# Half-block units in the first batch, an early 256 token filler job and a paced filler

## The chip, the cores and the metric

The kernel runs on one core of one Trainium2 chip. The core has TensorE (PE in the profile; PEld is its weight load), VectorE (DVE), ScalarE (ACT), GpSimd (POOL) and SyncE (SP), which here only issues DMAs. The metric is the device time of one execution in microseconds.

## The reference

Three layers, one after the other, on float32 data: windowed attention with a linear distance bias (4 batches, 8 heads, 576 tokens, head size 64, window 128), a gated layer with a 1536 wide inner dimension, and a layer with a cosine gate, 2048 wide inside. The model width is 512, the tokens are 2304.

```python
scores = scale * q @ k.T ;  mask = (rel >= 0) & (rel < 128)
attn = softmax(where(mask, scores - slope[h] * abs(rel), -1e9))
x = (attn @ v)                                  # to 2304 x 512
g = x @ w_gate ; x = (silu(g) * (x @ w_val)) @ w_out
h = x @ w_in2 ;  out = (h * cos(h)) @ w_out2
```

## The kernel before

Products of the two later layers are made of three matmuls of a high and a low part (`mm3`, lines 80 to 83, and 972 to 974), 128 rows deep, with the tokens as columns. The inputs come as 64 bit floats; each weight tile is converted on the core (`convert`, lines 100 to 177: ScalarE lines 127 and 129, VectorE 130, 137, 138, 142, GpSimd or ScalarE for the high part, GpSimd 164 for the low part).

**Attention** is a loop over item slots `n` (lines 638 to 702). A unit is a pair of heads of one batch, 16 units in all, four to a batch (`NP`). A unit has nine items: two heads times four blocks of 128 queries, and one item for the last 64 tokens of both heads (`i == NB`). Items go through stages at fixed lags in slots: scores (`do_s`, PE line 473), bias and row minimum (`do_bias`, VectorE 481), exponential (`do_exp`, ScalarE 490), reciprocal of the sum (VectorE 496, 501), scaling (`do_norm`, GpSimd 514), transposition (`do_t`, PE 533 or 523), copy of the transposed block (`do_hi`, ScalarE 551 or VectorE 554, 555), the product with v (`do_pv`, PE 587, tail 565 and 567). The result goes to `xh` and `xl` (ScalarE 592, 574; VectorE 593, 576), 512 tokens at a time, the tail separately. Two items at a time make a group. Every engine works through its instructions in the order in which this loop gives them out; `post` holds what is given out one slot later.

Units are prepared one ahead: q and k of the next unit are transposed on PE through the one bank `pq` (line 410, also used by the tail of the product with v), copied out by VectorE (416) and ScalarE (419, 430, 432). Their loads (line 352, 357) and those of v (368, 372) are issued by SyncE in the order of the loop; v's tile has two buffers, so a load of v waits in SyncE's queue for the unit two before.

**The filler** puts the first part of the gated layer, 3 of its 12 column tiles (`F0`), between attention work. When the last unit of a batch is done, `release(b)` (line 291) is called, which happens at slot 42 for batch 0. `filler` then yields one step of three matmuls at a time, two jobs of 288 tokens for each batch. A job has 12 gate steps, 12 value steps (`a_l1`, evacuations in lines 238 to 264) and 12 output steps (`a_l2`, written out by line 284), with the output steps of a job behind the gate steps of the next. `run_fill` takes 1.6 steps a slot (`RATE`). What is left after the attention stage runs in lines 976 to 983.

**After that** come the rest of the gated layer (lines 1019 to 1047) and the cosine layer (lines 1179 to 1217). In the latter, each product bank is emptied by `take` (VectorE line 1113, ScalarE 1123), and `slot_chains` moves each living chain (`cosine`, lines 1084 to 1104) one step: ScalarE, a VectorE pair (1091, 1092), ScalarE, GpSimd 1097, ScalarE, a subtraction (1103). In the first three steps `take` stands ahead of the chains.

## Time and profile before

| | us |
|---|---|
| median of 3 runs | 991.73 |
| lowest, highest | 990.09, 994.07 |
| the profiled execution | 992.14 |
| its span, first to last instruction | 990.4 |
| mean granted TensorE clock in it | 0.987 |

The profile is of one execution. Busy time of an engine is the time in which it has an instruction under way; matmuls overlap, so a busy PE need not be at its peak, and the granted clock (1.00 is 2.4 GHz, 0.50 is 1.2 GHz, values between are means over both) says how fast it ran. The views used are the page (busy time, slices), windows (busy time by stretch), timelines of one engine, groups of instructions and the issues of DMAs. In a timeline the bracket gives the idle time of the engine ahead of the instruction and what ended it.

### The profile page before, as it was taken

The page shows a single profiled execution, that of the slowest core. Times are in us where ns is not written, and L with a number is a line of the kernel's source. Part 1 is how long each engine was busy: PE and PEld are TensorE (multiplying, and loading weights), DVE is VectorE, ACT ScalarE, POOL GpSimd, SP SyncE. Part 2 cuts the span into 40 slices and gives each one's busy share as a digit, 9 for nine tenths or more (in the row PEclk, how much of TensorE's full clock was granted, in tenths as well). Part 3 has the DMA queues.
Part 4 walks back from the last instruction along what each step waited for, and adds up shares of the span by engine and source line. Part 5 has one row for each costly group of instructions (what it writes and reads, how often), then busy time and mean ns, then how long its engine had stood idle before and what let it go on. Part 6 is the DMA issues. An engine that isn't in the chain of part 4 may idle for free.

```text
span 990.4 us, 17037 instructions
## 1 busy us (share of the span) xinstructions
PE 967.4 (98%) x5616; PEld 887.2 (90%) x5616; DVE 737.3 (74%) x1548; ACT 594.4 (60%) x1365; POOL 483.1 (49%) x567
## 2 busy tenths in 40 slices
PE   6789999999999999999999999999999999999998
PEld 4558888889999999999999999888889888898886
DVE  6867777766288989989989755789666796666664
ACT  6876676644254545555455433877677776776663
POOL 5656556652245667769678721544222342223221
PEclk9879999999999999999999999999999999999999
DMA  7642333322383647547557525865767656676552
GB/s 180 154 98 61 97 81 77 84 80 70 107 282 107 203 128 232 194 137 249 168 171 243 195 91 173 281 198 183 242 199 230 199 163 199 187 240 201 165 176 85
DMA packets 145159, 163.65 MB, mean 165 GB/s; under 512 B 64688, under 2 KB 105648, under 8 KB 144816
## 3 DMA queue, kind: packets, MB, share of 16 engines
q1 hardware_dynamic: 143872, 162.27, 52.6%
q8 instruction: 45, 0.74, 0.3%
q10 hardware_dynamic: 1200, 0.30, 0.1%
q14 instruction: 42, 0.34, 0.1%
HBM read 126.88 MB, written 35.65 MB: 164 GB/s over the span
## 4 chain that ended last, share of the span: by engine, by line
PE 93%; DVE 2%; ACT 1%; issue 1%; POOL 1%; SPq 1%; DMA 1%; POOLq 0%; DVEq 0%
PE l L81 13%; PE l L83 13%; PE l L82 13%; PE pm L81 9%; PE pm L82 8%; PE pm L83 8%; PE pm L972 5%; PE pm L974 5%; PE pm L973 5%; PE s L473 4%; PE pv L587 3%; PE pq L410 1%; PE t L533 1%; PE t L523 1%; DVE r L1092 1%
## 5 line engine op out<-in xcount | busy, mean ns | idle before, releaser
L1097 POOL TENSOR_TENSOR r<-r,c 128x384 f32<-128x384 f32 x96 | 104.6, 1091 | 250.9 <-ACT r L1095 171.2
L81 PE MATMUL pm<-xh,wh 128*128 128x384 f32 (+1 forms) x452 | 151.7, 336 | 0.0
L83 PE MATMUL pm<-xh,wl 128*128 128x384 f32 (+1 forms) x452 | 144.9, 321 | 0.0
L82 PE MATMUL pm<-xl,wh 128*128 128x384 f32 (+1 forms) x452 | 144.9, 320 | 0.0
L81 PE MATMUL l<-wo,hh 128*128 128x512 f32 x288 | 114.0, 396 | 0.0
L82 PE MATMUL l<-wo,hh 128*128 128x512 f32 x288 | 113.5, 394 | 0.0
L83 PE MATMUL l<-wo,hl 128*128 128x512 f32 x288 | 113.5, 394 | 0.0
L972 PE MATMUL pm<-xh,ws 128*128 128x384 f32 x318 | 107.8, 339 | 0.8 <-DVE q L1113 0.7
L793 POOL TENSOR_TENSOR cs<-cs,st 128x512 uint32<-128x512 uint32 x56 | 80.3, 1433 | 56.6 <-DVE cs L791 47.0
L974 PE MATMUL pm<-xh,ws 128*128 128x384 f32 x318 | 107.7, 339 | 0.0
L973 PE MATMUL pm<-xl,ws 128*128 128x384 f32 x318 | 107.2, 337 | 0.0
L514 POOL TENSOR_SCALAR e<-e,st 128x128 f32<-128x128 f32 (+1 forms) x144 | 60.2, 421 | 60.3 <-DVE st L501 45.0
L81 PEld LDWEIGHTS pm<-xh,wh 128*128 128x128 f32 x452 | 85.3, 189 | 3.6 <-issue 3.0
L82 PEld LDWEIGHTS pm<-xl,wh 128*128 128x128 f32 x452 | 85.4, 189 | 0.0
L83 PEld LDWEIGHTS pm<-xh,wl 128*128 128x128 f32 x452 | 85.2, 188 | 0.0
L1087 ACT ACTIVATE a<-c 128x384 f32<-128x384 f32 x96 | 49.7, 517 | 53.2 <-DVE c L1113 53.2
L490 ACT ACTIVATE e<-e,st 128x256 f32<-128x256 f32 (+1 forms) x144 | 68.0, 474 | 18.8 <-DVE st L481 13.5
L1092 DVE SCALAR_TENSOR_TENSOR r<-a,r 128x384 f32<-128x384 f32 x96 | 76.8, 800 | 3.3
L1094 ACT ACTIVATE r<-r 128x384 f32<-128x384 f32 x96 | 50.4, 525 | 44.0 <-DVE r L1092 43.9
L81 PE MATMUL l<-uh,wh 128*128 128x384 f32 x216 | 72.8, 337 | 0.2 <-DVE acc L918 0.2
L83 PE MATMUL l<-uh,wl 128*128 128x384 f32 x216 | 72.6, 336 | 0.0
L82 PE MATMUL l<-ul,wh 128*128 128x384 f32 x216 | 72.5, 336 | 0.0
(179 smaller groups left out, 2624.0 us busy)
## 6 DMA issues: line engine op xcount, KB each, us to landing
ws<-wid SPq DMA_DIRECT2D x168, 256.0 KB, 2.8
wo<-wod SPq DMA_DIRECT2D x48, 512.0 KB, 4.8
st<-in_moe_w_out_dram SPq DMA_DIRECT2D x28, 512.0 KB, 3.8
st<-in_moe_w_in_dram SPq DMA_DIRECT2D x16, 512.0 KB, 3.8
st<-in_moe_w_gate_dram SPq DMA_DIRECT2D x12, 512.0 KB, 4.0
st<-in_moe_w_val_dram SPq DMA_DIRECT2D x12, 512.0 KB, 4.0
wid<-sh SPq DMA_DIRECT2D x24, 256.0 KB, 4.2
wid<-sl SPq DMA_DIRECT2D x24, 256.0 KB, 4.0
```

The lines of the kernel that those rows point to most:

```text
L81: nc.tensor.matmul(out=ps, lhsT=ah, rhs=bh, start=start, stop=False)
L82: nc.tensor.matmul(out=ps, lhsT=ah, rhs=bl, start=False, stop=False)
L83: nc.tensor.matmul(out=ps, lhsT=al, rhs=bh, start=False, stop=stop)
L490: nc.scalar.activation(out=e[:, :w], in_=e[:, :w], func=AF.Exp, bias=st[:, m:m + 1], scale=-1.0, accum_out=st[:, 2 + 2 * m:3 + 2 * m])
L514: nc.gpsimd.tensor_scalar(e[:, :w], e[:, :w], st[:, 8 + 2 * m:9 + 2 * m], 1.0, ALU.mult, ALU.mult)
L793: nc.gpsimd.tensor_tensor(out=ti, in0=ti, in1=st[:, :, 0], op=ALU.add)
L972: nc.tensor.matmul(out=o, lhsT=wh, rhs=xh_, start=start and kk == 0, stop=False, skip_group_check=True)
L973: nc.tensor.matmul(out=o, lhsT=wh, rhs=xl_, start=False, stop=False, skip_group_check=True)
L974: nc.tensor.matmul(out=o, lhsT=wl, rhs=xh_, start=False, stop=kk == 1, skip_group_check=True)
L1092: nc.vector.scalar_tensor_tensor(out=r, in0=a, scalar=-C2, in1=r, op0=ALU.mult, op1=ALU.add)
L1094: nc.scalar.activation(out=r, in_=r, func=AF.Abs)
L1097: nc.gpsimd.tensor_tensor(out=r, in0=r, in1=h, op=ALU.mult)
```

## The change

In batch 0, units 1, 2 and 3 are cut in two: blocks 0 and 1 of the three units come first (items 9 to 20), then blocks 2 and 3 with the tail (items 21 to 35). The number of items and slots stays. The product with v of a half covers only its columns, 256 tokens at a time, and a unit's chunk is marked in `ready` when the first 256 tokens are there. The filler's first job has 256 tokens and begins with two gate tiles at once, chunk by chunk as `ready` says; the last chunk comes at item 29, after which it goes on with gate and value steps, and with output steps if all its inputs are there. The second job of batch 0 has the other 320 tokens and waits for the release. `rate` spreads the steps that are left up to the next release.

The lags for transposing, copying and the product with v become 4, 5 and 6 slots for the first halves and unit 3, and 5, 6 and 7 for the second halves of units 1 and 2. Loads and preparation get slots of their own (`Q0`, `K0`, `TT0`, `LQ`, `LV`); units 2 and 3 are loaded and prepared earlier. The tiles for v, q, k and the tails have four buffers. The tail product of units 2 and 3 goes to the pool `pm` (before, that of unit 3 alone). In the cosine layer, `take` of steps 0 to 2 moves behind the chains, as in the later steps, and the subtraction of step 0 moves from GpSimd to VectorE.

```diff
+    ready = set()
     def a_l1(job, nm, fs, st):
-        b, hf = job
-        tok = slice(b * S + hf * HT, b * S + (hf + 1) * HT)
+        t0, nt = job
+        tok = slice(t0, t0 + nt)
+        if t0 == 0 and nm == "g":
+            two = [bank() for _ in range(2)]
+            for kk in range(KD):
+                while kk not in ready or ("g", 1) not in g0:
+                    yield "wait"
+                c = slice(kk * 128, (kk + 1) * 128)
+                for f in range(2):
+                    wh, wl = g0["g", f]
+                    mm3(two[f][:, :nt], wh[:, c], wl[:, c], xh[:, kk, tok], xl[:, kk, tok], kk == 0, kk == KD - 1)
+                    if kk == KD - 1:
+                        post.append(lambda f=f: evac_l1("g", f, st, two[f], nt))
+                    yield
+            fs = fs[2:]
...
-                mm3(ps[:, :HT], wh[:, c], wl[:, c], xh[:, kk, tok], xl[:, kk, tok], kk == 0, kk == KD - 1)
+                mm3(ps[:, :nt], wh[:, c], wl[:, c], xh[:, kk, tok], xl[:, kk, tok], kk == 0, kk == KD - 1)
                 if kk == KD - 1:
-                    post.append(lambda ps=ps, f=f: evac_l1(nm, f, st, ps))
+                    post.append(lambda ps=ps, f=f: evac_l1(nm, f, st, ps, nt))
...
     def filler():
         prev = None
         for b in range(B):
-            while released[0] < b:
-                yield "wait"
-            for hf in range(2):
+            cut = HA if b == 0 else HT
+            for hf, job in enumerate(((b * S, cut), (b * S + cut, S - cut))):
                 st = {}
-                job = (b, hf)
+                while b + hf > 0 and released[0] < b:
+                    if prev and "ready" in prev[1]:
+                        yield from a_l2(*prev)
+                        prev = None
+                    else:
+                        yield "wait"
                 yield from a_l1(job, "g", range(F0), st)
                 if prev:
...
+    filled = [0]
+    STEPS = 2 * 3 * F0 * KD
+    def rate(n, due):
+        b = released[0]
+        if released[0] < 0 or b + 1 == B:
+            return RATE
+        return min(RATE, max(STEPS * (b + 1) - filled[0] - due, 0) / max((b + 2) * NP * NI + PVS + 2 - n, 1))
...
-    nat2 = att.enter_context(tc.tile_pool(name="nat2", bufs=2))
-    qk_p = att.enter_context(tc.tile_pool(name="qk", bufs=2))
+    nat2 = att.enter_context(tc.tile_pool(name="nat2", bufs=4))
+    qk_p = att.enter_context(tc.tile_pool(name="qk", bufs=4))
...
-    vtail = [const.tile([128, 2, D], F32, name=f"vtail{j}") for j in range(3)]
+    vtail = [const.tile([128, 2, D], F32, name=f"vtail{j}") for j in range(4)]
...
-    items, first, final = [], {}, {}
-    for u in range(U):
-        for i in range(0, NB, 2):
+    items, first, final, part, scores = [], {}, {}, {}, {}
+    HB = NB // 2
+    order = [(0, 0, NB + 1)] + [(u, *c) for c in ((0, HB), (HB, NB + 1)) for u in range(1, NP)]
+    for u, b0, b1 in order + [(u, 0, NB + 1) for u in range(NP, U)]:
+        base = len(items)
+        for i in range(b0, min(b1, NB), 2):
             for h in range(2):
                 items += [(u, h, i), (u, h, i + 1)]
-        items.append((u, 0, NB))
-        for j in range(0, NI, 2):
-            g = list(range(u * NI + j, u * NI + min(j + 2, NI)))
+        if b1 > NB:
+            items.append((u, 0, NB))
+        count = len(items) - base
+        for j in range(0, count, 2):
+            g = list(range(base + j, base + min(j + 2, count)))
             first[g[0]] = final[g[-1]] = g
+            part[g[-1]] = b0, b1
+            ahead = j if j == count - 1 else j // 4 * 4
+            scores.setdefault(base + ahead - (1 if ahead == j == count - 1 else 0), []).append(g)
...
-            ps = (pm.tile([128, 512], F32, tag="pm", name="pm") if u == NP - 1 else
+            ps = (pm.tile([128, 512], F32, tag="pm", name="pm") if NP - 2 <= u < NP else
                   ps_q.tile([128, 512], F32, tag="pq", name="pq"))[:, :128]
...
+        lo, hi = part[n][0] * 128, min(part[n][1], NB) * 128
+        begun = True
         for j in range(NB):
-            c = slice(j * 256, min(j * 256 + 256, NB * 256 - 128))
-            o = slice(j * 128, j * 128 + c.stop - c.start)
+            o = slice(max(j * 128, lo), min(j * 128 + 256, hi))
+            if o.start >= o.stop:
+                continue
+            c = slice(o.start + j * 128, o.stop + j * 128)
             for x in range(2):
                 nc.tensor.matmul(out=ps[64 * x:64 * x + 64, o], lhsT=v[:, j, x], rhs=pth[u, x][:, c],
-                                 start=j == 0, stop=True, skip_group_check=True)
+                                 start=begun, stop=True, skip_group_check=True)
+            begun = False
 
         def fin():
-            tok = slice(b_ * S, b_ * S + NB * 128)
-            nc.scalar.copy(out=xh[:, p, tok], in_=ps)
-            post.append(lambda: nc.vector.tensor_tensor(
-                out=xl[:, p, tok], in0=ps, in1=f32(xh[:, p, tok]), op=ALU.subtract))
+            tok = slice(b_ * S + lo, b_ * S + hi)
+            nc.scalar.copy(out=xh[:, p, tok], in_=ps[:, lo:hi])
+            def low():
+                nc.vector.tensor_tensor(out=xl[:, p, tok], in0=ps[:, lo:hi], in1=f32(xh[:, p, tok]), op=ALU.subtract)
+                if lo == 0 and b_ == 0:
+                    post.append(lambda: ready.add(p))
+            post.append(low)
         post.append(fin)
...
     RATE = 1.6
     EXP, NORM, TRANS, HIGH, PVS = 2, 2, 5, 6, 8
-    AHEAD = {0: (0, 2), 4: (4, 6), 7: (8,)}
-    Q0, K0, TT0 = 2, 5, 4
+    Q0, K0, TT0 = {1: 2, 2: 9, 3: 13, 4: 28}, {1: 5, 2: 11, 3: 15, 4: 31}, {1: 4, 2: 10, 3: 14, 4: 30}
+    LQ, LV = {2: 1, 3: 6, 4: 20, 5: 33}, {1: 7, 2: 10, 3: 14, 4: 34}
+    for u in range(NP + 1, U):
+        Q0[u], TT0[u], K0[u] = ((u - 1) * NI + j for j in (2, 4, 5))
+        LV[u] = (u - 1) * NI + 7
+        if u + 1 < U:
+            LQ[u + 1] = (u - 1) * NI + 6
+    Q0, K0, TT0, LQ, LV = ({n: u for u, n in t.items()} for t in (Q0, K0, TT0, LQ, LV))
     due = pdue = 0.0
 
-    def last_pair(n):
-
-        return 0 <= n < N and items[n][0] == NP - 1
-
-    def staged(n, late, early):
-
-        if last_pair(n - early) and n - early in final:
-            return final[n - early]
-        return None if last_pair(n - late) else final.get(n - late)
+    def lag(n):
+        u, _, i = items[n]
+        if u in (0, *range(NP, U)):
+            return TRANS, HIGH, PVS + (i == NB)
+        if u == NP - 1 or part[n][0] == 0:
+            return TRANS - 1, HIGH - 1, PVS - 2
+        return TRANS, HIGH, PVS - 1 + (u == 1 and i == NB)
+    def staged(n, stage):
+        for j in range(TRANS - 1, PVS + 2):
+            if n - j in final and lag(n - j)[stage] == j:
+                return final[n - j]
+        return None
...
-        due += 0.7 * RATE
-        u, idx = divmod(n, NI)
-        v1 = u + 1 if u + 1 < U else None
+        pace = rate(n, due)
+        due += 0.7 * pace
...
-        if u < U and idx in AHEAD:
-            do_s([first[u * NI + j] for j in AHEAD[idx]])
-        turned, high = staged(n, TRANS, 4), staged(n, HIGH, 5)
+        if n in scores:
+            do_s(scores[n])
+        turned, high = staged(n, 0), staged(n, 1)
...
-        for m in first.get(n if idx == NI - 1 else n - 1, ()) if idx else ():
-            do_bias(m)
+        for m in [*first.get(n - 1, ()), *first.get(n, ())]:
+            if (items[m][2] == NB) == (m == n):
+                do_bias(m)
...
         due -= run_fill(int(due))
-        due += 0.3 * RATE
-        for back in (PVS + 1, PVS, PVS - 2):
-            for m in (ended(back) or ())[-1:]:
-                u_, h_, i_ = items[m]
-                if (h_ == 1 and i_ == NB - 1 or i_ == NB) and back == (
-                        PVS - 2 if last_pair(m) else PVS if i_ == NB - 1 else PVS + 1):
-                    do_pv(m)
-        if v1 is not None:
-            if idx == Q0 + 1:
-                prep_q(v1)
-            if idx == Q0:
-                prep_t(v1, "q")
-            if idx == K0:
-                prep_t(v1, "k")
-            if idx == K0 + 1:
-                prep_k(v1)
-            if idx == TT0 + 1:
-                prep_tail(v1)
-            if idx == max(TT0, K0) + 1:
-                load_qk(u + 2)
-            if idx == 7:
-                load_v(u + 1)
+        due += 0.3 * pace
+        valued = staged(n, 2)
+        if valued and (items[valued[-1]][2] == NB or items[valued[-1]][1] == 1 and
+                       items[valued[-1]][2] == min(part[valued[-1]][1], NB) - 1):
+            do_pv(valued[-1])
+        for at, act in ((n - 1, prep_q), (n, prep_t)):
+            if at in Q0:
+                act(Q0[at], "q") if act is prep_t else act(Q0[at])
+        if n in K0:
+            prep_t(K0[n], "k")
+        if n - 1 in K0:
+            prep_k(K0[n - 1])
+        if n - 1 in TT0:
+            prep_tail(TT0[n - 1])
+        if n in LQ:
+            load_qk(LQ[n])
+        if n in LV:
+            load_v(LV[n])
...
-        (nc.gpsimd if k == 0 else nc.vector).tensor_tensor(out=lo, in0=r, in1=f32(hi), op=ALU.subtract)
+        nc.vector.tensor_tensor(out=lo, in0=r, in1=f32(hi), op=ALU.subtract)
         HS[k, fi, half] = hi, lo
...
-    def slot_chains(chains):
-
-        for c in chains:
+    def slot_chains(most):
+        for c in list(live)[:most]:
             if next(c, "end") == "end":
                 live.remove(c)
...
-            chains = list(live)[:2 if k < 2 else 99]
-            if k < 3:
-                take(k, m, ps)
-            slot_chains(chains)
+            slot_chains(2 if k < 2 else 99)
             flush()
             if bg:
                 bg.popleft()()
-            if 2 < k < K2:
+            if k < K2:
                 take(k, m, ps)
             for _ in range(PER[m]):
```

## Rows read from the trace of the kernel before

**Rows 1.** Page: busy time and share; granted clock in 40 slices of 24.8 us.

```profile
PE 967.4 (98%) x5616; PEld 887.2 (90%) x5616; DVE 737.3 (74%) x1548; ACT 594.4 (60%) x1365; POOL 483.1 (49%) x567
...
PEclk9879999999999999999999999999999999999999
```

**Rows 2.** Windows: stretch, its length, busy per engine (instructions), PEclk, DMA, GB/s.

```profile
19.10:45.10 26.00, 22.62 (x129) 15.39 (x128) 22.07 (x78) 22.60 (x70) 20.87 (x30) 0.80 0.58 147
...
48.00:71.70 23.70, 20.25 (x108) 13.13 (x109) 15.98 (x61) 16.20 (x50) 14.17 (x22) 0.71 0.42 106
...
71.70:212.00 140.30, 140.28 (x1099) 120.37 (x1098) 105.66 (x437) 93.51 (x330) 82.43 (x193) 1.00 0.35 87
```

**Rows 3.** The same view, two stretches of 2 us.

```profile
32.00:34.00 2.00, 0.39 (x4) 0.18 (x3) 0.99 (x5) 1.94 (x8) 1.92 (x4) 1.00 0.77 151
...
68.00:70.00 2.00, 2.00 (x12) 1.06 (x10) 0.45 (x2) 0.00 (x0) 1.42 (x4) 0.50 0.00 0
```

**Rows 4.** Timeline of PE: start, us, line, operation, out<-in, count [idle before <-releaser].

```profile
33.87 0.63 PE L410 MATMUL pq<-ident,q 128*128 128x128 f32 x4 [1.61 <-issue]
...
45.08 0.93 PE L473 MATMUL s<-kx,qx 64*128 64x128 f32 x8
...
67.39 3.26 PE L587 MATMUL pv<-pth,v 128*64 128x256 f32 x16
...
71.70 0.38 PE L81 MATMUL pm<-xh,wh 128*128 128x288 f32 x1
...
75.07 1.32 PE L473 MATMUL s<-kx,qx 64*128 64x128 f32 x8
...
88.03 0.93 PE L473 MATMUL s<-kx,qx 64*128 64x128 f32 x8
```

**Rows 5.** Timeline of GpSimd: the last early weight.

```profile
66.98 1.27 POOL L164 TENSOR_TENSOR wl<-ct,wh 128x512 fp32r<-128x512 f32 x1 [0.19 <-ACT wh L171]
```

**Rows 6.** Timeline of PE: filler steps, first matmuls of the first and ninth.

```profile
229.18 0.30 PE L81 MATMUL l<-xh,wh 128*128 128x288 f32 x1
...
232.34 0.29 PE L81 MATMUL pm<-xh,wh 128*128 128x288 f32 x1
```

**Rows 7.** Timeline of SyncE's queue: issues.

```profile
12.63 0.37 SPq L92 DMA_DIRECT2D st<-in_moe_w_gate_dram  x1
...
13.10 1.24 SPq L352 DMA_DIRECT2D q<-in_q_dram  x2
...
17.39 1.19 SPq L368 DMA_DIRECT2D v<-in_v_dram  x2
```

**Rows 8.** DMA view, 0 to 80 us: issues, KB, median us to landing.

```profile
st<-in_moe_w_gate_dram SPq DMA_DIRECT2D x3, 512.0 KB, 4.2
```

**Rows 9.** Timeline of ScalarE: second gate weight taken up.

```profile
18.45 0.68 ACT L127 ACTIVATE ct<-st 128x512 f32<-128x512 f32 x1
```

**Rows 10.** Groups, 72 to 212 us: count | busy us, mean ns | idle.

```profile
L249 DVE SCALAR_TENSOR_TENSOR fu<-th,fu 128x288 f32<-128x288 f32 x15 | 6.7, 450 | 0.0
...
L246 ACT ACTIVATE th<-fu 128x288 f32<-128x288 f32 x15 | 6.5, 435 | 0.2
...
L244 ACT ACTIVATE fu<-pm 128x288 f32<-128x288 f32 x15 | 6.1, 407 | 2.3 <-PE pm L83 2.0 <-DVE st L481 0.2
...
L257 DVE TENSOR_TENSOR fu<-fu,pm 128x288 f32<-128x288 f32 x12 | 5.2, 432 | 0.0
```

**Rows 11.** Timeline of VectorE: the subtraction that empties bank pq.

```profile
33.31 0.46 DVE L576 TENSOR_TENSOR xl<-pq,xh 64x64 fp32r<-64x64 f32 x2 [0.86 <-ACT xh L574]
```

**Rows 12.** Timeline of PE's weight loads: all three with idle, 603 to 642 us.

```profile
612.08 0.19 PEld L972 LDWEIGHTS l<-xh,ws 128*128 128x128 f32 x1 [0.41 <-DVE c L1113]
...
620.47 0.19 PEld L972 LDWEIGHTS l<-xh,ws 128*128 128x128 f32 x1 [1.13 <-DVE c L1113]
...
632.27 0.19 PEld L972 LDWEIGHTS pm<-xh,ws 128*128 128x128 f32 x1 [1.11 <-DVE q L1113]
```

**Rows 13.** Timeline of VectorE: one of a chain's pair.

```profile
626.95 0.55 DVE L1091 SCALAR_TENSOR_TENSOR r<-a,c 128x384 f32<-128x384 f32 x1
```

53 lines of the change are left out of this document (27 added, 26 removed).

## The prediction

> **What bounds the kernel now.** I read the page first, then busy time by stretch, then TensorE's own instructions in order of time, then the queues beside it. TensorE is busy for 967.4 us of the 990.4 us span [rows 1], so the reader should look for the few places where it is not working at full clock. They are nearly all at the start. From 71.7 to 212 us PE is busy for 140.28 of 140.3 us at a granted clock of 1.00, and the clock stays there to the last slice but one [rows 1, 2]. Before 71.7 us it is different: from 48 to 71.7 us the mean clock is 0.71, which between the two levels of 2.4 and 1.2 GHz means 58% of that stretch at 1.2 GHz. The pattern is a stretch in which PE hardly works (0.39 of 2 us) followed by full busy time at clock 0.50 [rows 3].
>
> The boundary at 71.7 us is the first filler matmul: batch 0 is released at item slot 42, and only then has PE more work than it can do [rows 4]. Slots can be placed by each unit's first score matmuls, nine slots apart: unit 3 (slot 27) at 45.08, unit 5 (slot 45) at 75.07, unit 6 at 88.03 us [rows 4]. So a slot costs 1.53 to 2.0 us before the release and 12.96 / 9 = 1.44 us after it. From the release on, the end is PE work plus nothing, so each us of PE work done before the release comes off the end, and each us by which the release slips is added.
>
> **Part 1, the early job.** By the code, half-block units release the chunks of the 256 tokens at slots 18, 21, 25 and 29: two steps each at first, then the rest at 1.6 a slot. The gate of one chunk needs three slots after its last step, so value steps start at slot 32 and the 24 gate and value steps are done at about slot 39. The 12 output steps need the last output weights, whose final subtraction ran at 66.98 us [rows 5], and are entered two slots later, at slot 42, the release itself. So 24 steps move, not 36. A step of three 288 column matmuls takes 0.395 us (eight steps from 229.18 to 232.34 us, [rows 6]); with 256 columns in proportion 0.351 us. 24 x 0.351 = **-8.4 us**. The second job has 320 columns instead of 288, which gives the columns back; nothing is saved there.
>
> **Part 2, when the release comes.** I split the way to it in two.
>
> Slots 9 to 28, 19.1 to 48 us: ScalarE is busy 22.60 and VectorE 22.07 of 26 us [rows 2], so what they must wait for counts. SyncE's queue is the first cost. The loads of unit 2's q and k, six issues from 13.10 to 17.39 us, now stand ahead of the gate weight load that is issued at 12.63 us [rows 7]. That load needs 4.2 us to land [rows 8], so at present it is there at 16.8 us, and ScalarE takes it up at 18.45 us out of unbroken work [rows 9]. Delayed by 4.3 us with 1.65 us to spare, it holds ScalarE, and the exponentials queued behind it, for about 2.6 us; ends 0 (the six issues fit in a pause of the queue) and 4.3; I take 2.5. Unit 3's loads go ahead of the next weight in the same way; that is in the upper end. Against it, value loads have four buffers and wait for nobody. Three more casts and three more subtractions (halves of 256 columns) have no row of their own; the nearest, 0.41 to 0.45 us for 288 columns [rows 10], bounds them at 1.3 us on each engine; the full ones they shorten give part back: +0.8. K of units 2 and 3 is now copied one slot before its scores read it, where three slots lay between; PE waits at both places, 0 to 1 us each: +0.5. A gain: the 1.61 us gap before the q transposes at 33.87 us [rows 4] ends when the subtraction of the attention tail has left the one pq bank at 33.77 us [rows 11]; the transposes of units 2 and 3 now run before such a tail, and later tails use another pool. ScalarE works through most of that gap (1.94 of 2 us, [rows 3]), so I count 1.0 of 1.6. Together **+2.8 us** (0 to 7).
>
> Slots 29 to 42, 48 to 71.7 us, 23.7 us: ScalarE needs 16.2 us and VectorE 16.0 [rows 2]. The moved gate and value evacuations add 3 x (0.41 + 0.435) = 2.5 to ScalarE and 3 x (0.45 + 0.43) = 2.6 to VectorE [rows 10], which makes 18.7 and 18.6 us. PE at full clock needs per slot 1.44 - 1.6 x 0.395 = 0.81 us for attention, 10.5 us for 13 slots, plus 18 steps x 0.351 = 6.3: 16.9 us. All three fit in the 23.7 us; what fills it now is the low clock and waits, such as the last value product, 3.26 us for 16 matmuls [rows 4]. With filler in PE's waits the clock should hold. At ScalarE's 87% of the first stretch, 18.7 us become 21.5: **-2.2 us** (-5 if packed, +10 if cold, below).
>
> **Part 3, the pacing.** After the release the rate is (72 - 24 done) over the 40 slots to the next release, 1.2 instead of 1.6. PE then needs 0.81 + 1.2 x 0.395 = 1.28 us a slot; VectorE has 105.66 / 140.3 x 1.44 = 1.08 us [rows 2], a little less with fewer steps. PE stays the bound by 0.2 us a slot, but no longer with a queue that hides everything. No row shows this load; the nearest on one side is no idle at all (0), on the other the slot that stays at 1.44 us, 40 x 0.165 = 6.6. I take the PE-bound side, at **+1.0 us**.
>
> **Part 4, the cosine stage.** In its first three steps the bank of a product is emptied behind the chains' VectorE pairs instead of ahead of them, and one subtraction per chain of step 0 goes from GpSimd to VectorE. PE's weight loads wait there three times now, from 0.41 to 1.13 us [rows 12], each for such an addition. One pair is 2 x 0.55 us [rows 13], so at most 3 x 1.1 = 3.3 us more, at least nothing (no matmul waits for the moved subtractions, which excludes a gain); half, **+1.6 us**.
>
> **The sum**: -8.4 + 2.8 - 2.2 + 1.0 + 1.6 = -5.2. The profiled execution took 992.14 us, 0.4 above the median of 991.73, so 986.9 for a like execution and **986.5 us** at the median. The whole gain is at the edge of what a measurement can tell from no change, about 0.5% or 5 us.
>
> **Rivals.** B, the start packs: SyncE's crowding is hidden and the two gaps at the pq bank go, so slots 9 to 28 cost nothing more, slots 29 to 42 take 19.2 us and pacing leaves no idle: -8.4 - 4.5 + 1.6 = -11.3, 980.4 us. For it: ScalarE and VectorE use only 68% of 48 to 71.7 us. Against: they are at 85 to 87% before it.
>
> C, the early steps run cold, and it ends slower. PE has in slots 29 to 42 16.9 us of work at 2.4 GHz; at 1.2 GHz it is 33.8 us, 10 more than the stretch has now: -8.4 + 2.8 + 10 + 1.0 + 1.6 = +7.0, 998.7 us. It decides from 26.7 us of stretch, that is when about three fifths of that work run at the low level. For it: the clock was at 0.50 for PE work that filled its time [rows 3], so being busy did not at once bring it back. Against: from 71.7 us on, the same filler brought 1.00 at once and kept it [rows 2]. The Trainium skill (TensorE: Matmul & The Clock Gate, section "HAM oscillation — how this bites in real kernels") speaks for C: bursts shorter than the waits between them are throttled again each time. By that rule the two-step bursts at slots 18, 21 and 25 warm nothing and C's time would follow; rows of 32 to 70 us agree that the low level follows a near-idle stretch, but none shows filler there.
>
> D, the pace opens idle time: slots 43 to 82 stay at 1.44 us because chains of VectorE, ScalarE and GpSimd set them. Then 5.6 us more than I counted: +0.4, 992.1 us. For it: PE was never short of work there, so nothing shows that the chains alone are faster.
>
> E, the early job does less than it says because silu or weights come later than my slot count; for each step not moved 0.35 us is lost. Half of them would give -1.0, 990.7 us.
>
> **Chances.** Forecast 0.50 (983 to 990.5 by itself), B 0.20, D 0.13, C 0.10, E 0.07. Faster by over 0.5% (below 986.8): B and a little over half of the forecast, 0.50. Slower by over 0.5%: C and the worst ends of parts 2 and 4, 0.13. Within: 0.37. The range of 979 to 994 takes in B and D, and leaves out C and B's best end.
>
> **What would show it.** Part 1: 72 matmuls of 256 columns by gate and value weights before the score matmuls of slot 42, and output steps only after. Part 2: the first 288 or 320 column filler work, or the tail product of unit 3, near 72 us; a ScalarE wait for the second gate weights near 19 us; a clock well above 0.71 from slot 29 on. Part 3: PE busy over 97% to the next release, with slots near 1.28 us. Part 4: waits of PE's weight loads in the first steps that grow by one to two us in all. I would be wrong in the mechanism if the release comes over 4 us later, and in the size if PE is idle for several us between the first two releases.

## The result, and the profile after

The changed kernel is slower. Its median is 997.53 us (six runs, 995.95 to 999.57) against 991.94 for the kernel before on the same chip (six runs, 990.09 to 994.07): a ratio of 1.0061, interval 1.0049 to 1.0072. The forecast was 986.5 us. The profiled execution took 998.07 us, with a span of 996.2.

Four landmarks divide the difference of the two profiled executions (start of the named matmul, us):

| | before | after | difference |
|---|---|---|---|
| unit 3's tail product, with which batch 0 is released | 70.91 | 74.92 | +4.0 |
| first 384 column matmul, the attention stage is over | 262.52 | 267.61 | +5.1 |
| first product of the cosine layer | 603.42 | 609.45 | +6.0 |
| end of the span | 990.4 | 996.2 | +5.8 |

So 4 us come ahead of the release. The first row is one execution of each kernel: two runs further down that have the changed kernel's instructions up to the release put it at 75.24 and 77.35 us. From the release to the end of the attention stage, where the forecast had 7.4 us less (24 steps, 8.4 us, less 1.0 of idle time), it takes 1.1 us more. The stages after it are nearly as long as before.

The page of after answers [rows 1]:

```profile
PE 968.1 (97%) x5628; PEld 888.1 (89%) x5628; DVE 738.2 (74%) x1558; ACT 595.2 (60%) x1368; POOL 478.7 (48%) x563
...
PEclk9899999999999999999999999999999999999999
```

No engine has more than 0.9 us more to do; TensorE's busy time is the same within 0.7 us. Windows of after, for the stretches of [rows 2] by slots (9 to 28, 29 to the release, from there on); the columns are those of [rows 2]:

```profile
19.10:51.70 32.60, 26.18 (x159) 18.18 (x159) 25.80 (x86) 24.83 (x77) 23.11 (x32) 0.84 0.51 135
51.70:75.60 23.90, 20.88 (x173) 17.44 (x172) 19.51 (x70) 19.47 (x62) 16.24 (x25) 1.00 0.41 98
75.60:216.00 140.40, 137.21 (x1025) 115.89 (x1024) 100.78 (x422) 89.14 (x316) 78.90 (x186) 0.99 0.34 84
```

The clock from slot 29 to the release is 1.00, where it was 0.71; whether the early steps do that is asked of the next runs. But the stretch ahead of it has grown, and after the release TensorE is no longer busy throughout (137.2 of 140.4 us).

TensorE's timeline of after, answering [rows 4]: its four longest waits in the attention stage from slot 9 on, the tail product (unit 3's is the one that releases batch 0), the first filler matmul after the release.

```profile
24.53 1.11 PE L442 MATMUL pq<-ident,k 128*128 128x128 f32 x4 [3.02 <-DVE qx L448]
...
46.55 0.39 PE L84 MATMUL pm<-xl,wh 128*128 128x256 f32 x1 [1.31 <-DVE xl L640]
...
55.18 0.38 PE L83 MATMUL pm<-xh,wh 128*128 128x256 f32 x1 [1.80 <-ACT fu L262]
...
74.92 0.39 PE L607 MATMUL pm<-ptt,vtail 128*128 128x128 f32 x2
...
75.99 0.42 PE L83 MATMUL pm<-fh,wh 128*128 128x256 f32 x1
...
118.89 0.42 PE L83 MATMUL pm<-fh,wh 128*128 128x320 f32 x1 [1.48 <-POOL fh L276]
```

The first filler matmul after the release reads `fh`: an output step, as the forecast said. The four waits are read further down. None of them explains the drift after the release. That shows on VectorE, in the groups of five whole units (10 to 14, from scores to scores), first before, then after:

```profile
L481 DVE CUSTOM_DVE_ANT_0 e<-s,rel 128x256 f32<-128x256 f32 (+1 forms) x40 | 14.2, 387 | 1.7 <-PE s L473 0.9 <-PE t L523 0.5
```

```profile
L521 DVE CUSTOM_DVE_ANT_0 e<-s,rel 128x256 f32<-128x256 f32 (+1 forms) x40 | 14.6, 387 | 7.8 <-PE s L513 7.4 <-PE t L563 0.2
```

Forty bias instructions, as long each; but VectorE stands idle ahead of them for TensorE's scores (the name after the arrow) for 7.4 us instead of 0.9. The windows of these units, before and after:

```profile
137.87:201.49 63.62, 63.62 (x502) 54.71 (x501) 48.16 (x197) 41.59 (x147) 37.32 (x88) 1.00 0.33 81
```

```profile
143.67:208.92 65.25, 65.12 (x503) 55.69 (x502) 47.26 (x197) 41.81 (x148) 37.22 (x87) 1.00 0.30 73
```

They hold all but the same matmuls (502 and 503, with 24 output steps and 48 others of the filler in both), at full clock, with PE busy for all but 0.13 us, and yet the second takes 1.6 us longer. The view of waits lists none of TensorE in either.

The cause is one line of the diff that the forecast passed over. Before, both items of a pair are biased in the second item's slot, the first item ahead. The new loop looks at each item by itself, `(items[m][2] == NB) == (m == n)`: the second item of a pair is now biased in the first item's slot, and the first one slot later. In every other pair that is the slot in which TensorE issues these scores, so VectorE, which works in order, waits for them ahead of work that was ready.

### The profile page after: what moved, and what is told of

The parts are those of the page before. It is cut to its first block, busy times and chain, and to the rows that moved or that the text cites. A ratio compares the mean times of both kernels' runs of the same rounds, so it can differ in the third digit from the quotient of the medians.

```text
span 996.2 us, 17019 instructions
## 1 busy us (share of the span) xinstructions
PE 968.1 (97%) x5628; PEld 888.1 (89%) x5628; DVE 738.2 (74%) x1558; ACT 595.2 (60%) x1368; POOL 478.7 (48%) x563
## 4 chain that ended last, share of the span: by engine, by line
PE 88%; DVE 5%; ACT 3%; DMA 1%; issue 1%; POOL 1%; SPq 0%; POOLq 0%; DVEq 0%; ACTq 0%
PE l L83 13%; PE l L85 13%; PE l L84 13%; PE pm L83 8%; PE pm L84 8%; PE pm L85 8%; PE pm L1028 5%; PE pm L1030 5%; PE pm L1029 5%; PE s L513 4%; PE pv L631 2%; PE pq L442 1%; PE t L563 1%; ACT e L530 1%; PE t L573 1%
## 5 line engine op out<-in xcount | busy, mean ns | idle before, releaser
L83 PE MATMUL pm<-xh,wh 128*128 128x384 f32 (+3 forms) x452 | 152.2, 337 | 1.9 <-ACT fu L262 1.8
L84 PE MATMUL pm<-xl,wh 128*128 128x384 f32 (+3 forms) x452 | 144.9, 321 | 1.4 <-DVE xl L640 1.3
L85 PE MATMUL pm<-xh,wl 128*128 128x384 f32 (+3 forms) x452 | 144.8, 320 | 0.0
L554 POOL TENSOR_SCALAR e<-e,st 128x128 f32<-128x128 f32 (+2 forms) x144 | 61.0, 428 | 74.6 <-DVE st L541 55.4
L530 ACT ACTIVATE e<-e,st 128x256 f32<-128x256 f32 (+2 forms) x144 | 67.9, 473 | 32.5 <-DVE st L536 17.2
```

What stands on the lines that cost most here:

```text
L83: nc.tensor.matmul(out=ps, lhsT=ah, rhs=bh, start=start, stop=False)
L84: nc.tensor.matmul(out=ps, lhsT=ah, rhs=bl, start=False, stop=False)
L85: nc.tensor.matmul(out=ps, lhsT=al, rhs=bh, start=False, stop=stop)
L530: nc.scalar.activation(out=e[:, :w], in_=e[:, :w], func=AF.Exp, bias=st[:, m:m + 1], scale=-1.0, accum_out=st[:, 2 + 2 * m:3 + 2 * m])
L554: nc.gpsimd.tensor_scalar(e[:, :w], e[:, :w], st[:, 8 + 2 * m:9 + 2 * m], 1.0, ALU.mult, ALU.mult)
```

## The experiments

Each ratio is to the kernel before, timed on the same chip beside the run. "Pairs" is the edit of the run of that name below.

### One part of the change at a time

The first four keep the line.

**Half blocks alone**: the early job, its two-tile branch and the pacing are taken out.

```diff
-        if t0 == 0 and nm == "g":
+        if False:
...
-                while b + hf > 0 and released[0] < b:
-                    if prev and "ready" in prev[1]:
-                        yield from a_l2(*prev)
-                        prev = None
-                    else:
-                        yield "wait"
+                while released[0] < b:
+                    yield "wait"
...
-        if released[0] < 0 or b + 1 == B:
-            return RATE
+        return RATE
```

> The changed kernel with the half-block order, the new preparation slots and the cosine order kept, but no filler before the release and the old constant rate of 1.6: the filler's first job waits for batch 0. This prices the reordering alone. Theory R (the reordering itself holds the release back): the scores of unit 4 (slot 36) start 4 to 5 us later than in the kernel before (58.85 us), as in the changed kernel (64.0), and the end is 3 to 5 us later than before. Rival S (the early filler steps, in the way of the attention's matmuls, hold the release back): unit 4 within 1 us of 58.85, the end within 1 us of before.

Measured: 997.16 us, ratio 1.0062 (1.0044 to 1.0080). The tail product came at 70.34 us, 0.6 earlier than before, and the attention stage still ended 3.6 us late (266.14 us). Unit 4's first scores stand at 60.59 us, 1.7 later than before, which is neither of the two expectations. A loss that begins after the release and has nothing to do with the filler's early job or its rate: this run pointed to the line.

It shows a second thing. From slot 29 (scores at 51.27 us) to the tail product the granted clock is 0.98 without any early step, and the stretch is 19.1 us long:

```profile
51.27:70.34 19.07, 15.68 (x111) 10.91 (x111) 16.95 (x63) 16.32 (x53) 14.37 (x20) 0.98 0.51 122
```

In the changed kernel, with 18 early steps in it, it is 23.2 us (51.71 to 74.92). So in this execution the order of the blocks alone has the clock up and the stretch short, and the early steps lengthen it again by 4.1 us.

**Output steps kept back** behind the next release.

```diff
-                    if prev and "ready" in prev[1]:
+                    if b == 0 and prev and "ready" in prev[1]:
...
-        return min(RATE, max(STEPS * (b + 1) - filled[0] - due, 0) / max((b + 2) * NP * NI + PVS + 2 - n, 1))
+        return min(RATE, max(STEPS * (b + 1) - F0 * KD - filled[0] - due, 0) / max((b + 2) * NP * NI + PVS + 2 - n, 1))
```

> The changed kernel, but output steps are never run ahead of a release after the first: from batch 1 on the filler waits for the release, so the second job's output steps come behind the next job's gate steps as in the kernel before; the pace aims at 12 steps fewer for that. Theory B (output steps directly behind value steps make TensorE wait for GpSimd's high and low parts at the boundary of batches 0 and 1, and the clock falls for it): slots 72 to 81 take 11 to 12 us instead of 15.45, and the end is 3 to 4.5 us earlier than the changed kernel. Rival P (the lower pace itself opens the idle time there, the wait only takes its place): the idle time moves to another place in units 5 to 8 and the end is within 1 us of the changed kernel.

Measured: 996.81 us, ratio 1.0059 (1.0039 to 1.0078). The wait at 118.89 us is gone and the end has not moved: the theory that it costs 3 to 4.5 us is wrong.

**Cosine layer as before.**

```diff
-        nc.vector.tensor_tensor(out=lo, in0=r, in1=f32(hi), op=ALU.subtract)
+        (nc.gpsimd if k == 0 else nc.vector).tensor_tensor(out=lo, in0=r, in1=f32(hi), op=ALU.subtract)
...
-            slot_chains(2 if k < 2 else 99)
+            chains = list(live)[:2 if k < 2 else 99]
+            if k < 3:
+                take(k, m, ps)
+            slot_chains(chains)
...
-            if k < K2:
+            if 2 < k < K2:
```

> The changed kernel with the cosine layer as in the kernel before (take ahead of the chains in steps 0 to 2, the subtraction of step 0 on GpSimd). Theory Z (that part of the change costs nothing: from the first product of the cosine layer to the end the two traces take 386.6 and 387.0 us): the same time as the changed kernel within 1 us. Rival, the prediction: 1.6 us (0 to 3.3) faster than the changed kernel.

Measured: 998.50 us, ratio 1.0072 (1.0054 to 1.0091). From the first cosine product to the end it takes 387.0 us, as before; in the changed kernel 386.8. Part 4 costs nothing. The waits that answer [rows 12], in the changed kernel:

```profile
618.37 0.19 PEld L1028 LDWEIGHTS l<-xh,ws 128*128 128x128 f32 x1 [0.68 <-DVE c L1169]
...
626.48 0.19 PEld L1028 LDWEIGHTS l<-xh,ws 128*128 128x128 f32 x1 [0.87 <-DVE c L1169]
...
633.24 0.19 PEld L1028 LDWEIGHTS pm<-xh,ws 128*128 128x128 f32 x1 [0.72 <-ACT q L1179]
```

**Queries and keys of units 2 and 3 turned earlier.**

```diff
-Q0, K0, TT0 = {1: 2, 2: 9, 3: 13, 4: 28}, {1: 5, 2: 11, 3: 15, 4: 31}, {1: 4, 2: 10, 3: 14, 4: 30}
+Q0, K0, TT0 = {1: 2, 2: 7, 3: 12, 4: 28}, {1: 5, 2: 10, 3: 15, 4: 31}, {1: 4, 2: 9, 3: 14, 4: 30}
```

> The changed kernel with q of unit 2 prepared two slots earlier (slot 7) and its k one (10), q of unit 3 one earlier (12). Theory Q (the one bank pq holds TensorE: the k transposes of unit 2 wait 3.0 us at 21.5 us because VectorE's copy of q out of pq stands behind a weight conversion, the clock falls to 0.50 from 24 to 31 us, and the 4 us of slip are there by slot 17): the wait goes, unit 3's first scores (33.95 us) come 2 to 4 us earlier and the end 1.5 to 4 us earlier. Rival D (VectorE and ScalarE set this stretch by their work, the wait is only their sign): unit 3's first scores within 1 us, the end within 1 us.

Measured: 997.34 us, ratio 1.0060 (1.0039 to 1.0080). Unit 3's first scores moved from 33.95 to 32.83 us, and the tail product stayed at 74.92: what the rival said, not the theory.

### The line

**Pairs**: the changed kernel with the old order, and nothing else.

```diff
-        for m in [*first.get(n - 1, ()), *first.get(n, ())]:
-            if (items[m][2] == NB) == (m == n):
-                do_bias(m)
+        for m in final.get(n, ()):
+            do_bias(m)
```

> The changed kernel with one line put back: VectorE biases both items of a pair in the second item's slot, the first item ahead of the second, as the kernel before does. The changed loop biases the second item one slot earlier, in the very slot in which TensorE issues its scores. Theory V (that line is what made the kernel slower): VectorE's idle time for scores falls back from 8.8 us in units 9 to 14 (131 to 205 us) to about 1, a steady unit with 14 filler steps goes from 12.98 us back to 12.56, eleven such units give back 4.5 us, the 4 us that the first batch slipped shrink by 1 to 3, and the time is 988.5 to 992, no longer slower than before (991.3 in this chip's earlier runs). Rival L (the loss is in the order of the half blocks and the pacing, and the line only moves idle time of an engine that is not the bottleneck): 996 to 998, steady units still 12.98.

**The line alone**: the kernel before with the new loop.

```diff
-        for m in first.get(n if idx == NI - 1 else n - 1, ()) if idx else ():
-            do_bias(m)
+        for m in [*first.get(n - 1, ()), *first.get(n, ())]:
+            if (items[m][2] == NB) == (m == n):
+                do_bias(m)
```

> The kernel before with that one line of the change alone: the second item of each pair is biased in its own slot, the first in the next. Everything else is the kernel before. Theory V: each unit of 12.56 us takes some 0.4 us more where the boundary between score banks is tight, about 15 units, so 4.5 to 6.5 us more than before: 996 to 998, with VectorE idle for scores some 8 us in 127 to 200 us where it was 0.9. Rival L: VectorE has slack (48 us busy of 64 in units 10 to 14), the end does not move: 991 to 992.5.

Measured: pairs 991.92 us, ratio 1.0001 (0.9991 to 1.0010); the line alone 997.81 us, ratio 1.0058 (1.0045 to 1.0071). Taken away it gives back 5.6 us at the median (997.53 to 991.92), put in alone it costs 6.1. That is the whole difference between the two kernels. VectorE's bias group in the same five units, in the run with pairs and in the run with the line alone:

```profile
L521 DVE CUSTOM_DVE_ANT_0 e<-s,rel 128x256 f32<-128x256 f32 (+1 forms) x40 | 14.2, 385 | 2.0 <-PE t L563 0.9 <-PE s L513 0.9
```

```profile
L481 DVE CUSTOM_DVE_ANT_0 e<-s,rel 128x256 f32<-128x256 f32 (+1 forms) x40 | 15.1, 386 | 8.7 <-PE s L473 8.4
```

And the windows of these five units, pairs, then the line alone:

```profile
141.20:204.70 63.50, 63.50 (x502) 54.62 (x501) 47.93 (x198) 41.66 (x148) 37.22 (x88) 1.00 0.31 75
```

```profile
139.04:205.07 66.03, 65.54 (x503) 55.83 (x502) 48.02 (x196) 41.47 (x147) 37.23 (x87) 1.00 0.32 78
```

0.5 us a unit. How a wait of VectorE, which is idle for some 15 of 64 us, comes to TensorE's time is seen in TensorE's own groups by form, pairs and then the line alone:

```profile
L513 PE MATMUL s<-kx,qx 64*128 64x256 f32 x60 | 8.7, 394 | 0.0
```

```profile
L473 PE MATMUL s<-kx,qx 64*128 64x256 f32 x60 | 10.3, 394 | 0.0
```

Sixty score matmuls, 394 ns each in both, but together they cover 8.7 us in one and 10.3 in the other: they overlap less. That is 1.6 of the 2.5 us; no other group of TensorE differs by more than 0.3, and it stands idle for 0.5. In the timeline eight of these matmuls of a unit take 1.13 us in the kernel before; in the changed one some take 1.17 and others 1.52. The group, and VectorE's last bias ahead of it, before and then after:

```profile
141.69 0.42 DVE L481 CUSTOM_DVE_ANT_0 e<-s,rel 128x256 f32<-128x256 f32 x1
...
142.64 1.13 PE L473 MATMUL s<-kx,qx 64*128 64x256 f32 x8
```

```profile
148.39 1.52 PE L513 MATMUL s<-kx,qx 64*128 64x256 f32 x8
...
148.43 0.28 DVE L521 CUSTOM_DVE_ANT_0 e<-s,rel 128x128 f32<-128x128 f32 x1
```

The two heads' matmuls alternate and go to two banks, and each bank has to be emptied by VectorE's bias of the pair before. VectorE now reaches the second bank later. In the five units of the two kernels with the line and of the two without it there are twenty such groups. The seven that take 1.31 to 1.56 us all begin before that last bias has ended; the other thirteen, of 1.13 to 1.17 us, all begin after it (by 0.37 us or more without the line). That TensorE waits for the bank in the midst of the eight is read from these times, which fit it without exception; the view of waits lists no such wait.

### The change without the line

**Half blocks with pairs** (both edits together).

> The half-block order with the pair line put back, and without the early filler job and the pacing: it prices the reordering alone, once the line is out. With the line as the change has it this took 997.2 us. Theory V: steady units back to 12.56, the drift after unit 5 gone, the time within 1.5 us of the kernel before (990 to 993), since unit 5 started 0.9 us earlier already. Rival L: 996 to 998.

**Pairs, output steps kept back** (both edits).

> The pair line put back and output steps kept behind the next release, as before (pace lowered by the 12 steps that then remain). Theory V together with the loss at the batch boundary (2 us of idle and a low clock, 115 to 131 us): 986 to 990, below the version with the line alone by up to 2 us. Rival P (the steps that do not run at the boundary leave TensorE idle in units 5 to 8 instead, 0.3 to 0.5 us each): the same as the version with the line alone, within 1 us, or slower.

Measured: half blocks with pairs 993.87 us, ratio 1.0024 (1.0014 to 1.0034); pairs with output steps kept back 991.38 us, ratio 0.9990 (0.9979 to 1.0002). With the line out the reordering alone costs 2.2 us, more than the 1.5 expected at most, and the early job with its pacing brings 2.0 of the 7.4 that the forecast gave it.

Why so little can be read from slot 29 to the tail product. Without early steps the stretch is 18.7 us long at a clock of 0.98; with them 24.3 in the run with pairs, and 22.8 with output steps kept back:

```profile
53.12:71.78 18.66, 15.65 (x112) 10.85 (x112) 15.27 (x55) 16.30 (x53) 14.08 (x19) 0.98 0.51 126
```

The 18 steps in it are 6.3 us of TensorE's work, and 4.1 to 5.7 us of that come back as a later release.

**Two waits taken out** of the early steps, on top of pairs. These are the waits at 46.55 and 55.18 us above: an early step is issued ahead of the low half that it reads, and the third gate tile is issued ahead of ScalarE's copy out of the first two tiles' banks. The edit issues each of them a slot or more later.

```diff
             fs = fs[2:]
+            while "free" not in st:
+                yield "wait"
...
             nc.scalar.activation(out=u, in_=ps[:, :nt], func=AF.Copy, scale=0.5)
+            if f == 1:
+                post.append(lambda: st.update(free=1))
...
-                    post.append(lambda: ready.add(p))
+                    post.append(lambda: post.append(lambda: ready.add(p)))
```

> The changed kernel with the pair line put back, and two waits of the early filler steps taken off TensorE: the third gate tile starts only in the slot after the copies out of the first two tiles' banks, and a token block counts as ready one slot later, when its low half is written. Theory W (the early steps cost what they wait for: 1.9 us for a bank and 1.2 us for a low half, in which VectorE and ScalarE starve, stand between the scores of slots 25 to 31): both waits gone from TensorE's list, two or three steps fewer ahead of the release (some 1 us later), so 1.5 to 3 us better than with the pair line alone (991.9): 989 to 990.5. Rival X (TensorE has no idle time left in slots 21 to 36, so the 24 steps cost their own 8 us wherever they stand): 991.5 to 993.

> The same with output steps kept behind the next release. Theory W: 1.5 to 3 us better than the pair line with output steps kept back (991.4): 988.5 to 990. Rival X: 991 to 992.5.

> The kernel of the run before it with unit 2's and unit 3's queries and keys turned one or two slots earlier. Unit 2's first scores stood at 26.9 to 27.3 us and unit 3's at 34 to 35, four slots each that took 4.9 us before the change. Theory Q (the chain of a unit's preparation, query transposes, VectorE's scaling, key transposes, ScalarE's copy, cannot be done in four slots): unit 3's first scores at 32 to 33, and the time 1 us below the run before it. Rival (what is won there is lost again by slot 26, as it was with the pair line still wrong): the same within 0.7 us.

Measured: 990.83 us, ratio 0.9995 (0.9984 to 1.0006); with output steps kept back 988.73 us, 0.9980 (0.9969 to 0.9991); with the earlier turns as well 989.28 us, 0.9975 (0.9964 to 0.9987). Both waits are gone. Against the same kernels with the waits the ratio falls by 0.0006 and, with output steps kept back, by 0.0010, that is 0.6 and 1.0 us for waits of 3.1 us in the profile, and the intervals overlap: a gain is likely but not shown. The 24 steps still lie ahead of the release, and the stretch from slot 29 to the tail product, 22.8 us, is no shorter than the 22.8 of the run with pairs and output steps kept back. The earlier turns change nothing clear of the intervals. The waits of TensorE from 38 to 66 us in the run with pairs, then in the run with the two waits out (waiter, released by: total, times, longest):

```profile
PE pm L83 <- ACT fu L262: 1.9, 1, 1.9
PE pm L84 <- DVE xl L640: 1.2, 1, 1.2
...
```

```profile
PE s L517 <- DVE st L525: 1.4, 2, 0.8
PE t L577 <- POOL e L558: 0.7, 2, 0.4
PE pq L609 <- ACT kx L455: 0.6, 1, 0.6
```

### The preparations of units 2 and 3

What the changed kernel loses up to slot 29 is lost by slot 17. VectorE's timeline of after, from unit 1's first scores on, up to the copy that the 3.02 us wait at 24.53 us is for:

```profile
20.99 1.49 DVE L139 TENSOR_SCALAR ct<-ct 128x512 uint32<-128x512 uint32 x1
22.51 0.84 DVE L140 SCALAR_TENSOR_TENSOR ct<-st,ct 128x512 uint32<-128x512 uint32 x1
23.28 0.28 DVE L521 CUSTOM_DVE_ANT_0 e<-s,rel 128x128 f32<-128x128 f32 x1
...
23.74 0.73 DVE L448 TENSOR_SCALAR qx<-pq,qscale 128x512 f32<-128x512 f32 x1
```

The query copy out of the one bank `pq` stands behind 2.3 us of weight conversion (`ct`); TensorE's key transposes need that bank. From 24.5 to 31 us, behind that wait, the granted clock is 0.50:

```profile
24.50:31.00 6.50, 6.32 (x28) 4.79 (x30) 4.36 (x12) 5.02 (x15) 3.54 (x4) 0.50 0.73 183
```

**Conversions later**: on top of pairs, none is started in slots 9 to 16; all later ones come eight slots later.

```diff
-        next(pieces, None)
+        if not 9 <= n < 17:
+            next(pieces, None)
```

> The changed kernel with the pair line put back and no weight conversion started in slots 9 to 16, so that all later ones come eight slots later. Theory K (unit 2's and unit 3's scores come 4 us late because VectorE's query scaling and ScalarE's key copy stand behind weight conversions, one of which waits for its weight's transfer): unit 3's first scores 2 to 4 us earlier than the 34 to 35 us of the runs with the line put back. The end need not follow, since the first steps of the early job then lack their weights: 990 to 995. Rival Q (the chain through the one bank for queries and keys is too long for four slots without any conversion): unit 3's first scores at 33.5 or later.

Measured: 988.92 us, ratio 0.9982 (0.9972 to 0.9992). Unit 3's first scores come at 32.05 us instead of 35.18 (33.46 to 35.67 in all runs with the conversions in their place and the turns not earlier), and TensorE's clock is 1.00 from 10 us on. To see whose cost that is, the same edit in other kernels:

> The kernel before with no weight conversion started in slots 9 to 16, all later ones eight slots later. Theory K (the conversions hurt only where three preparations are packed into slots 9 to 20): before has one preparation there, its unit 2 starts 0 to 1 us earlier, the release stays within 1 us, and the end is 990 to 992, like the kernel before. Rival S (conversions there are a loss in any order, and moving them is a gain that has nothing to do with the change): 2 to 3 us faster than before.

> The half-block order with the pair line put back, no early job, no pacing, and no weight conversion started in slots 9 to 16. Without the last it took 993.9 us, 2.2 more than before. Theory K: unit 3's first scores at 32 instead of 35.7 us and the time 2 to 3 us lower: 991 to 992, that is the reordering costs nothing once nothing stands ahead of the preparations. Rival (what is won at slot 17 is lost by the release): 993 to 994.5.

> The changed kernel with the pair line put back, the two waits of the early steps taken out, output steps kept behind the next release, queries and keys of units 2 and 3 turned earlier, and no weight conversion started in slots 9 to 16. If the terms add: the pair line and the waits with kept output steps gave 2.2 us below before, the moved conversions 2 to 3: 985 to 987, below both kernels, near the 5.2 us that the prediction had for the whole change. Rival (the early steps lack weights when conversions come later, and earlier preparations win nothing): 988 to 990.

> The same with queries and keys of units 2 and 3 turned in the changed kernel's own slots. With the conversions moved the chain has room, so the earlier turns should matter little: within 1 us of the run with them. If the chain itself is too long for four slots: 1 to 2 us slower.

| conversions later in | us | ratio to before (interval) |
|---|---|---|
| the kernel before | 986.80 | 0.9957 (0.9945 to 0.9968) |
| half blocks with pairs | 994.07 | 1.0021 (1.0010 to 1.0033) |
| all edits above | 989.87 | 0.9984 (0.9975 to 0.9992) |
| the same, turns not earlier | 988.69 | 0.9984 (0.9969 to 1.0000) |

My theory that only the packed preparations suffer from the conversions is wrong: the kernel before gains most, 4.5 us at the median. Its clock from 48 us to the release is 1.00, where it was 0.71, and the release comes 8 us earlier:

```profile
62.66 0.39 PE L567 MATMUL pm<-ptt,vtail 128*128 128x128 f32 x2
```

This version, the old order with eight slots without a conversion, beats both kernels, and none of the mended versions of the change comes to it at the median (the best interval, 0.9964 to 0.9987, touches its own). With the conversions out of the way the early job and its pacing are worth 3.9 us by the ratios (1.0021 with half blocks and pairs, 0.9982 with the whole change and pairs), twice what they brought before. There the stretch from slot 29 to the tail product takes 22.4 us at a clock of 0.77 without early steps and 22.6 at 1.00 with them: in this pair, of one execution each, the steps did fill what was lost, as forecast. But the mended terms do not add: with all edits TensorE is busy for only 55.9 of the 60 us after the release (60.0 before), one wait of 1.48 us there being for a value step's evacuation. The size of the edit was tried last, on the kernel before: slots 9 to 12 alone, and slots 9 to 22.

> The kernel before with no weight conversion started in slots 9 to 12. If the gain goes by the number of conversions that are moved behind the release (eight slots gave 4.3 us and a release 8 us earlier): about half, 988.5 to 990. If it is the place alone: the whole 4 us, 986 to 988.

> The kernel before with no weight conversion started in slots 9 to 22. If the gain goes by their number: 983 to 985. If the filler lacks its weights at the release, as 2.5 of the 8 us were already lost again with eight slots: 986 to 990, with idle time of TensorE behind the release.

Measured: 989.97 us, ratio 0.9983 (0.9974 to 0.9993), and 992.86 us, ratio 1.0011 (1.0003 to 1.0020). Four slots give 1.9 us, eight 4.5, and fourteen lose: with fourteen the tail product comes at 64.15 us, and the rest of the attention stage then takes 197.2 us (194.1 with eight, 191.6 in the kernel before). TensorE is busy there for only 18.26 of the 20 us from 72 on, at a clock of 0.91; with eight it is busy for all of them, at 1.00.

## Why the prediction was wrong

**The line within a pair** is in no term of the sum. I read the diff's loop over both slots' items as the old order written for units of any length. It costs 5.6 to 6.1 us, more than the whole gain that I forecast. The step that failed is the general argument, "from the release on, the end is PE work plus nothing": TensorE had the same matmuls, stayed busy, and was slower by 0.3 us a unit in the changed kernel and 0.5 with the line alone, since its scores waited for banks that VectorE emptied later.

**Without that line** the change is worth nothing (991.92 us against 991.69), where the sum had -5.2. By its terms:

- *Part 1, 24 steps, -8.4.* Right behind the release: 24 matmuls by `xh` and `wh` of 256 columns lie ahead of it, output steps only after it, and from the tail product to the end of the attention stage the run with pairs takes 186.1 us, the one without the two waits 184.6, against 191.6 before: -5.5 and -7.0, where parts 1 and 3 together gave -7.4. What was won there had been paid ahead of the release (slots 29 to 42 below).
- *Part 2, slots 9 to 28, +2.8.* Right in sum as far as single executions tell, wrong in its parts: +3.7 in the profile of after (19.1 to 51.7 us, where the forecast's stretch ended at 48), 1.6 to 6.1 in the other runs of this order with the conversions in their place and turns and early steps unchanged, and all of it in after by slot 17, whose scores stand at 33.95 us; before, those of slots 16 and 18 stand at 28.70 and 30.75. The step that failed is the preparations. I counted 0.5 us for the key copies and a gain of 1.0 at the `pq` bank; instead query and key both have to pass that bank in the four slots ahead of their scores, behind conversions, and a 3.02 us wait is the result. What I did charge, 2.5 us for SyncE's crowding, cost nothing: ScalarE takes up the second gate weight at 18.53 us, where it was 18.45 [rows 9]:

```profile
18.53 0.67 ACT L129 ACTIVATE ct<-st 128x512 f32<-128x512 f32 x1
```

- *Part 2, slots 29 to 42, -2.2.* The clock held, as forecast, so rival C was wrong where it was placed; but in the half-block order it held without the steps too (0.98), except with the conversions later (0.77). The time did not shrink (51.7 us to the tail product 23.2 us, and 22.9 from 48 us on before). I let the steps fill TensorE's waits and the low clock of the kernel before; the new order left little of either, 18.7 to 19.1 us without the steps, and with them it takes 22.8 to 24.3, with the conversions in their place. That is the step that failed, and by it most of part 1 was lost again. The steps' own waits, 1.8 us for a bank and 1.3 for a low half just ahead of slot 29, which I had not looked for, explain little of it: with both taken out the stretch is still 22.8 us long.
- *Part 3, +1.0.* About right: behind the release TensorE is busy for 58.3 of 60 us in the run with pairs and 59.5 in the one without the two waits (56.9 after). In the changed kernel the worst of its waits is the 2.0 us at the batch boundary, at 118.89 and 119.83 us; keeping output steps back took 0.2 us off there by the ratios, and 1.1 and 1.5 in the later runs.
- *Part 4, +1.6.* Wrong: nothing. The three waits are 0.68, 0.87 and 0.72 us where they were 0.41, 1.13 and 1.11 [rows 12].

The release was named as the test of the mechanism: wrong if over 4 us later. It was 4.0 us later after, 5.5 in the run with pairs, 3.0 without the two waits. These are single executions, and their clocks differ at 20 to 30 us (0.71, 0.50, 0.67), so only the sign is firm: runs with the same instructions up to the release put it at 74.92, 75.24 and 77.35 us with the line, and at 76.42 and 72.37 without it. One reading of the forecast is off without touching the sum: 1.53 to 2.0 us a slot holds for slots 27 to 42 only; slots 9 to 27 took 26 us, 1.44 a slot. On the Trainium skill's page (TensorE: Matmul & The Clock Gate, section "HAM oscillation — how this bites in real kernels") that I had weighed for rival C: the bursts of two steps did not run cold as a whole (clock 1.00 from 36 to 48 us in the profile of after). What it describes is there in another place, the 0.50 behind the wait at 24.53 us; in the run with pairs the clock is at 0.50 from 21 us on, ahead of the wait for the same copy, so that wait is not the only way there.

## What to carry to other kernels

A loop that is rewritten for another order has to be read for what it now issues in each slot, instruction by instruction and engine by engine, also for the units that are not meant to change; two waits per unit on an in-order engine with slack cost more here than everything that was expected of the change. When work is to fill idle time, ask whether that idle time is still there in the new order, by a run of the order without the work. And look first for what already stands in the way: holding back eight slots of weight conversions brought 4.5 us, with the old order.

## What the runs showed of the hardware

- Matmuls of 64 rows for two heads, alternating, overlap: eight of 394 ns each (256 columns) take 1.13 to 1.17 us when VectorE has emptied both banks ahead of them, and 1.31 to 1.56 when they begin before it has. PE reads as busy in both cases and no wait is listed; busy time of the group against its count shows the loss, and VectorE's times beside it the cause.
- VectorE's conversion instructions have no fixed length in the start: the same form, 128 x 512, took 0.40 to 1.49 us (line 139 of the changed kernel, nine of them up to 67 us). What stretches it, the traces don't settle.
- TensorE's clock at the start differs between executions of the same instructions: from 20 to 30 us it was 0.71, 0.67 and 0.52 in three runs that are alike up to the release, which came at 74.92, 77.35 and 75.24 us.
